# A hint at the head of every engine's program, for the branch over a fallback path

## The chip, the cores and the metric

The kernel runs on one core of one Trainium2 chip. A core has five engines that each run their own list of instructions: TensorE (PE in the profile), VectorE (DVE), ScalarE (ACT), GpSimd (POOL) and SyncE (SP).[...] The metric is the device time of one execution in microseconds (us), and the median over several runs counts.

## The reference

The first half is a linear attention with a complex, gated state. For each of 4 x 8 heads and each of 768 time steps, a state of 48 x 48 is multiplied by a complex gate of modulus at most 0.999, the outer product of a key and a value is added, and the query reads the real part:

```python
for t in range(S):
    new_re = ar * S_re - ai * S_im
    new_im = ar * S_im + ai * S_re
    S_re, S_im = (new_re + kv, new_im)
    y[:, :, t] = np.einsum('bhd,bhde->bhe', q[:, :, t], S_re)
```

The second half takes y as 3072 tokens of 384 numbers through a feed-forward layer with 2048 hidden numbers and the activation h * erf(softplus(h)):

```python
h = x @ w_in
sp = np.maximum(h, 0.0) + np.log1p(np.exp(-np.abs(h)))
g = h * erf(sp)
return (g @ w_out).astype(np.float32)
```

## The kernel before

The program holds two complete ways to the result. The fast one, `quotient_path` (line 682), replaces the recurrence by quotients of running products of the gates, so that it becomes matrix products; this is only good while certain sums over the data stay within limits. The general one, `product_path` (line 172), has no such condition. The fast path always runs. While it runs it collects sums into small tiles, and its step `check()` (line 1305) turns them into one integer, `ok`, which is 1 when all limits hold (the last operation is a reduction on DVE at line 1321). After the fast path every engine loads `ok` into a register (line 1388) and compares it (line 1389): if it is below 1, the general path runs and overwrites the output; otherwise the engines jump over it. With this input `ok` is 1, and none of the general path's instructions runs.

The fast path treats the tokens in 12 units of 256, each as two chunks of 128 rows. For a unit it loads gates, queries, keys and values, computes the gates' magnitudes, angles and decays, the scores and the state, then the first matrix product into `h` (line 1152), the activation (lines 786 and 1180 to 1186) and the second product (line 1220, and for the later units a form with seven instead of eight half-size products, line 1244). The result of a unit goes to the memory by two writes on SP's queue (line 1211). The order of all these steps is written out by hand in one long string, `ORDER` (line 49), and a scheduler leaves it as it is. It ends with the last products of unit 11 on PE, the last additions on DVE (line 1252) and the two last writes by SP; `check()` is spread over the last part of it.

At the head of the program the engines pass a barrier (line 1405), and then each begins its part of the fast path: SP and ACT issue the first loads (line 802), POOL builds an identity and a triangle, PE runs products of the identity with itself that nobody reads (line 1302).

In each engine's list the instructions stand in this order: the head, the fast path, the load of `ok` and the compare, the general path, a short piece for the other side of the condition, and the common end. The general path is 245 instructions on SP, 957 on ACT, 2537 on DVE, 743 on POOL and 4270 on PE. The short piece for the other side advances semaphores by what the general path would have added to them: one semaphore instruction on each engine but SP, and eight on SP, one for each semaphore that its transfers use. Each of these first waits until the fast path's own count is reached; SP's seventh is the one that the last write of the result increments. The common end (line 1416) has eight more semaphore waits on SP and two barriers in which POOL waits for the four other engines and releases them.

## Time and profile before

| what | value |
|---|---|
| median of 3 runs | 662.15 us (661.24 to 662.20) |
| profiled execution, its own time | 662.76 us |
| its span, from the first to the last instruction | 660.9 us |
| granted TensorE clock | 0.998 |
| busy share of the span: PE, DVE, ACT, POOL | 97%, 91%, 87%, 0% |

The span runs from the first to the last instruction of the program; what lies around it, 1.8 us, is the start and end of an execution. A busy time counts arithmetic only: semaphore instructions, register loads, branches and the issuing of transfers are listed as rows, with their times, but are not counted as busy. Engines' own instruction streams come through transfers too; the profile lists them as queues of the kind "instruction" (q8 and q14).

### The profile page before, as it was taken

The numbers are of one execution on the slowest core, as the hardware profiler recorded it, in microseconds if no ns is written. First come the engines' busy times: TensorE is split into PE (matmuls) and PEld (weight loads), VectorE is DVE, ScalarE is ACT, GpSimd is POOL, SyncE is SP. The second block draws the span as 40 slices with busy tenths as digits, with TensorE's granted clock in tenths as the row PEclk, the third lists the DMA queues.
The fourth block names the chain that finished last, engine by engine and source line by source line (L and its number), as shares of the span: only waits on it lengthen the run. The fifth ranks groups of instructions, "written<-read, shape, count | busy, mean of one in ns | idle before, by whom it ended". The sixth has DMA issues, their size and how long they took to land.

```text
span 660.9 us, 12302 instructions
## 1 busy us (share of the span) xinstructions
PE 642.7 (97%) x4728; PEld 562.4 (85%) x4728; DVE 603.3 (91%) x980; ACT 577.8 (87%) x762; POOL 1.1 (0%) x8
## 2 busy tenths in 40 slices
PE   7889999999999999999999999999999999999996
PEld 7678887777777877999899899999999899998886
DVE  4999999999999999999999999999999898877892
ACT  6999999999999999987978999997997886788810
POOL 0000000000000000000000000000000000000000
PEclk9999999999999999999999999999999999999999
DMA  8896785563157327328516726626637505511000
GB/s 197 202 266 155 188 168 120 137 127 61 24 88 132 61 37 183 70 41 199 97 17 162 145 42 151 121 39 153 119 58 144 127 16 128 136 37 48 1 25 30
DMA packets 282796, 70.23 MB, mean 106 GB/s; under 512 B 269396, under 2 KB 272488, under 8 KB 282728
## 3 DMA queue, kind: packets, MB, share of 16 engines
q1 hardware_dynamic: 280648, 68.96, 48.3%
q8 instruction: 39, 0.64, 0.4%
q10 hardware_dynamic: 2080, 0.39, 0.3%
q14 instruction: 29, 0.24, 0.1%
HBM read 48.82 MB, written 4.75 MB: 81 GB/s over the span
## 4 chain that ended last, share of the span: by engine, by line
ACT 47%; DVE 26%; PE 18%; DMA 4%; issue 4%; SPq 0%; ACTq 0%; DVEq 0%
ACT L785 10%; ACT yy L786 8%; PE hps L1152 8%; ACT z L786 7%; DVE z L1180 4%; DVE yy L1182 4%; ACT e L786 4%; DVE e L1184 4%; ACT y L786 3%; DVE h L1186 3%; ACT th L786 3%; ACT CS L786 3%; ACT h L1155 3%; PE Y L1244 2%; ACT s L786 2%
## 5 line engine op out<-in xcount | busy, mean ns | idle before, releaser
L1152 PE MATMUL hps<-xT,w_in_sb 128*128 128x256 f32 x1152 | 262.5, 381 | 1.5 <-ACT h L1155 1.5
L1152 PEld LDWEIGHTS hps<-xT,w_in_sb 128*128 128x128 f32 x1152 | 215.6, 190 | 34.8 <-ACT h L1155 4.0
L785 ACT ACT_TABLE_LOAD x94 | 120.6, 1283 | 3.6 <-issue 2.1
L1180 DVE TENSOR_TENSOR z<-z,yy 128x512 f32<-128x512 f32 x96 | 64.8, 686 | 15.8 <-ACT e L786 14.8
L786 ACT ACTIVATE e<-z 128x512 f32<-128x512 f32 x96 | 58.2, 628 | 22.1 <-DVE h L1186 21.6
L1182 DVE SCALAR_TENSOR_TENSOR yy<-z,yy 128x512 f32<-128x512 f32 x96 | 65.1, 687 | 1.7
L1186 DVE SCALAR_TENSOR_TENSOR h<-e,h 128x512 f32<-128x512 f32 x96 | 65.0, 685 | 1.1
L1220 PE MATMUL ops<-w_out_sb,h 128*128 128x384 f32 x192 | 65.7, 488 | 0.1
L1184 DVE TENSOR_TENSOR e<-e,yy 128x512 f32<-128x512 f32 x96 | 64.6, 685 | 1.1
L1155 ACT COPY h<-hps 128x512 f32<-128x512 f32 x96 | 54.6, 579 | 11.0 <-PE hps L1152 11.0
L1220 PEld LDWEIGHTS ops<-w_out_sb,h 128*128 128x128 f32 x192 | 35.7, 190 | 21.9 <-DVE w_out_sb L848 1.1
L786 ACT ACTIVATE z<-h 128x2048 f32<-128x2048 f32 x24 | 45.8, 1910 | 6.7 <-DVE seen L858 6.0
L1084 PEld LDWEIGHTS sc<-KQ 96*128 96x128 f32 x384 | 47.6, 192 | 4.4 <-issue 2.3
L1084 PE MATMUL sc<-KQ 96*128 96x128 f32 x384 | 48.9, 275 | 1.3 <-DVE KQ L1075 0.9
L786 ACT ACTIVATE z<-z 128x2048 f32<-128x2048 f32 x24 | 45.9, 1910 | 0.6
L786 ACT ACTIVATE yy<-yy 128x2048 f32<-128x2048 f32 x24 | 45.9, 1912 | 0.5
L786 ACT ACTIVATE yy<-z 128x2048 f32<-128x2048 f32 x24 | 45.8, 1908 | 0.4
L1139 PE MATMUL y<-A,v 128*32 128x128 f32 x768 | 33.4, 275 | 1.3 <-DVE A L1088 0.9
L1088 DVE TENSOR_TENSOR A<-sc,triu 128x512 f32<-128x512 f32 x48 | 31.9, 681 | 1.0 <-PE sc L1084 1.0
L1103 PEld LDWEIGHTS kv<-v,kt 128*96 128x96 f32 x320 | 29.7, 165 | 1.5 <-issue 0.7
L1103 PE MATMUL kv<-v,kt 128*96 128x48 f32 x320 | 29.7, 246 | 0.0
L1244 PE MATMUL Y<-T,S 128*128 128x192 f32 x144 | 26.7, 331 | 1.8 <-DVE out L1252 1.3
(115 smaller groups left out, 1053.7 us busy)
## 6 DMA issues: line engine op xcount, KB each, us to landing
KQ<-X SPq DMA_DIRECT2D x240, 64.0 KB
raw<-in_moe_w_in_dram SPq DMA_DIRECT2D x8, 768.0 KB
raw<-in_moe_w_out_dram SPq DMA_DIRECT2D x8, 768.0 KB
again<-in_moe_w_in_dram SPq DMA_DIRECT2D x8, 768.0 KB
ar<-in_a_re_dram SPq DMA_DIRECT2D x24, 192.0 KB
k<-in_k_dram SPq DMA_DIRECT2D x24, 192.0 KB
q<-in_q_dram SPq DMA_DIRECT2D x24, 192.0 KB
v<-in_v_dram SPq DMA_DIRECT2D x48, 96.0 KB
```

Of the source, the lines that this page charges most:

```text
L785: scalar.preload_act_table_set(sets[0])
L786: scalar.activation(func=func, **kw)
L1084: nc.tensor.matmul(out=ps[:, j, :], lhsT=head("k", g * HG + j, u, c), rhs=head("q", g * HG + j, u, c), start=True, stop=True)
L1103: nc.tensor.matmul(out=kv[0:D2, j, :], lhsT=T["kt", u, c][:, j].rearrange("p u d -> p (u d)"), rhs=side(T["v", u][:, c, j // 2], j % 2), s ...
L1152: nc.tensor.matmul(out=ps[:, e, :], lhsT=w_in_sb[:, (sl * SLAB + i) // 2, kd, e * P:(e + 1) * P], rhs=T["xT", u][:, kd, :], start=(kd == 0 ...
L1155: scalar.copy(out=T["h", u, sl][:, i:i + 2, :], in_=ps)
L1180: vector.tensor_tensor(out=z, in0=z, in1=y, op=OP.mult)
L1182: vector.scalar_tensor_tensor(out=y, in0=z, scalar=-2.0, in1=y, op0=OP.add, op1=OP.mult)
L1184: vector.tensor_tensor(out=e, in0=e, in1=y, op=OP.mult)
L1186: vector.scalar_tensor_tensor(out=h, in0=e, scalar=1.0 / RT2, in1=h, op0=OP.add, op1=OP.mult)
L1220: nc.tensor.matmul(out=ps, lhsT=lhsT, rhs=w_out_sb[:, i, :], start=i == HALF, stop=i == KF - 1)
L1244: nc.tensor.matmul(out=ps, lhsT=a(sl)[:, i], rhs=b(sl, i), start=sl == 0 and i == 0, stop=sl == NSL - 1 and i == HALF - 1)
```

## The change

Two lines are added ahead of the load of `ok`, and the condition gets a label that ties them to it:

```diff
         quotient_path(tc, q, k, v, a_re, a_im, w_in, w_out, out, ok)
+        engines = [getattr(mybir.EngineType, e) for e in ("PE", "DVE", "SP", "Activation", "Pool")]
+        tc.mark_branch_hint_location("general", hint="LikelyTaken", engines=engines)
         fine = nc.values_load(ok[0:1, 0:1], min_val=0, max_val=1)
-        with tc.If(fine < 1):
+        with tc.If(fine < 1, label="general"):
             product_path(tc, q, k, v, a_re, a_im, w_in, w_out, out)
```

Each of the five engines gets one more instruction, a branch prefetch hint that names its own compare at the end of the fast path and says that the branch there is likely taken. Although the line stands behind the fast path in the source, the built program has the hint right after the barrier at the head, as the first instruction of each engine's part, ahead of the first load on SP and ACT, of the first product on PE and of the first write on DVE and POOL. No other instruction is added, removed or put in another order.

## The prediction

> **What bounds the kernel now.** A branch matters where it is executed, so I read the end of the span first: the chain of waits for its last piece, then the rows of the compare's line, then SP's own waits, then the transfers in the gap that these show.

> The chain, in order of time (start, length, what), for the last 31 us:

> ```profile
> span 660.9 us, 12302 instructions
> ...
> 654.29 1.31 PE W L1244 x8
> 655.60 0.02 issue
> 655.62 0.36 DVE out L1252
> ```

> The last arithmetic ends at 655.98, but the span ends at 660.9 (660.94 in the trace): 4.96 us follow that hold no arithmetic. The rows of line 1389, with durations in ns and the first and last start in us, show what is there:

> ```profile
> L1389 SPq EVENT_SEMAPHORE  x8: 17/17/17, 659.0 to 659.6; - x8
> L1389 ACTq COMPARE_BRANCH  x1: 50/50/50, 647.7 to 647.7; - x1
> ...
> L1389 ACTq EVENT_SEMAPHORE  x1: 17/17/17, 650.1 to 650.1; - x1
> ...
> L1389 PEldq COMPARE_BRANCH  x1: 3302/3302/3302, 653.1 to 653.1; - x1
> L1389 DVEq COMPARE_BRANCH  x1: 72/72/72, 656.4 to 656.4; - x1
> L1389 SPq COMPARE_BRANCH  x1: 50/50/50, 656.4 to 656.4; - x1
> ...
> L1389 DVEq EVENT_SEMAPHORE  x1: 21/21/21, 659.5 to 659.5; - x1
> ```

> SP's compare takes 50 ns, from 656.392, and its next instruction starts at 659.029: 2.59 us of nothing. On ACT the hole is 2.40 us (647.74 to 650.15), on DVE 3.09 (656.45 to 659.54); on PE it lies inside the compare's 3.30. SP's waits say the same, put down to SP itself, and the transfers between 656.4 and 659.03 show what fills the hole (queue, packets, MB, share):

> ```profile
> SPq L1389 <- SPq L1389: 2.6, 1, 2.6
> ```

> ```profile
> q8 instruction: 1, 0.02, 2.1%
> q14 instruction: 2, 0.02, 1.5%
> ```

> The two q14 packets are 8 KB each, at 657.41 and 657.70, 0.97 and 1.25 us behind the compares of SP and DVE; the two engines go on 1.28 and 1.52 us after these have landed. That is the branch's target being fetched. From there on SP sets the end: eight semaphore instructions, eight waits, two barriers, 659.03 to 660.94. ACT, POOL and PE have branched before (650.1 to 656.4) and wait for SP in the barrier.

> [...]

> **The change, part by part.** *Five hints at the head.* No row shows one.[...] I take 0.07 us, what SP needs from one semaphore instruction to the next (659.443 to 659.508). Nothing hides it: the chain starts with ACT's load of ai, issued at 0.80 right behind the barrier, and the first ACT operation waits for a load until 4.13. From there to 655 the order is fixed and PE is 97% busy, so a late start is a late end: +0.07[...]. On POOL the hint delays the identity and with it PE's unread products; on DVE a few memsets: not on the chain.

> *The fetch that moves.* If the hint brings the target in ahead of the branch, the holes close. Is there time? [...]between 624.6 and 647.7 q14 has no packet at all[...], 23 us ahead of the first branch; PE's block before the branch came at 638.96 on q8, 14 us ahead of its compare. A target fetch takes 0.3 to 1 us. POOL's hint is 13 rows ahead of its compare and has 647 us.

> *What stands behind the hole.* SP would go on at about 656.50 in place of 659.03, but that 2.5 us isn't the gain. Its eight instructions each wait for a transfer count, and the seventh is that of the last write, issued at 656.008: its 16 increments come from 657.78, fourteen by 657.91, the last two at 658.02 and 658.17. In the run before, this instruction started at 659.508, the write long finished. After the change it would start some 0.04 after the landing, at 658.21. All that follows (the eighth, the eight waits, the barriers: 659.508 to 660.942 = 1.43 us) keeps its length, since [...]DVE, now on from 656.5, is ahead of it. So the span ends at 658.21 + 1.43 = 659.64: -1.30 us. If the landing improves, more: the write issued 1.1 us before had all increments after 1.845 us, this one after 2.158, and an 8 KB fetch of 0.33 us runs beside its last packets. Without such a collision the landing is 0.31 earlier. But the resumed engines will at once fetch the block behind the target (SP did so 0.58 us after resuming, at 659.61): at some 657.1, again beside the write. Bounds 0 and -0.31; I take -0.10. A fetch of 8 KB earlier in the span costs nothing that shows: q14 moves 29 packets in 660 us, a share of 0.1% of the engines' time.

> *What else.* [...] The 1.8 us around the span stays.

> Sum against the profiled execution: -1.30 - 0.10 + 0.07 = -1.33; its span 660.94 becomes 659.6, its own time 662.76 becomes 661.4. The median of the runs shown is 0.61 below that time; the same step from 662.15 gives **660.8 us**, with 660.5 (-1.61) and 661.0 (-1.19) as the bounds of the sizes. The three runs of before lie 0.96 apart, so I put 0.3 around these: 660.2 to 661.3.

> **Rivals.** *The hint does not reach its branch.* Between the head and the branches q8 fetches 37 blocks and q14 21; if one of these fetches makes an engine forget it, all holes stay and the hint's 0.07 is paid: 662.2. For it: nothing in the profile shows a hint that lives so long. Against: the hint names its compare, so it has what it needs to be used only there.

> *It works on SP and not on DVE.* Then DVE still goes on at 659.54, and SP's sixth wait of the end (for DVE's count, 659.96 before) is released at 659.60 in place of 659.96: -0.36, with the head 661.9. For it: DVE comes to its branch last (its load of ok waits for the last addition), against: 23 us are enough for both.

> *Slower: the fetch at once.* If the hint fetches the target as soon as it is read[...], the first crossing of a block behind the head misses and pays what a miss costs here: 2.4 us on ACT, 3.1 on DVE. The first 40 us are a chain of ACT operations without slack, so one of these is exposed in full[...]: 662.15 + 0.07 + 2.4 = 664.6; with DVE's behind it 667.7. It decides from a stall of 1.3 us on, the gain at the end. For it: the hint stands as far from the branch as it can[...].

> **How the numbers follow.** This kernel's runs tell a change from none at about 0.2%, 1.32 us. The chances: it works, 0.74; works only in part, 0.05; is lost, 0.09; slower, 0.12. The worked case lies right on that mark (-1.33): with bounds of -1.61 and -1.19 and the runs' spread, I give 0.48 to beyond it and 0.26 to short of it. So faster 0.48; within 0.2%: 0.26 + 0.05 + 0.09 = 0.40; slower 0.12. The range takes in the worked case and both cases without effect, 660.2 to 662.4, and leaves out the slower one.

> **What would show it.** Right: on line 1389 SP's semaphore instructions begin at about 656.5, some 0.1 behind its compare, with a hole in the middle of the eight until 658.2 that waits for the write; PE's compare drops from 3302 ns to some 50; the q14 packets between 656.4 and 659 belong to the block behind; first loads issued at 0.87. Lost: line 1389 as before. At once: a gap of some 2.5 us on ACT or DVE in the first 70 us, with an early extra q14 packet. I'd be wrong in size if the end of the span depends on more than the write, for example if the engine's next block is needed before the barrier and comes late.

## The result, and the profile after

The changed kernel takes 660.43 us (median of 19 runs, 659.06 to 661.52), the kernel before 661.98 us (19 runs, 660.91 to 663.02). The ratio is 0.9976, with a 95% interval of 0.9969 to 0.9983: 1.55 us lie between the medians, a little over 0.2%. The forecast was 660.8 us.

The profiled execution takes 659.36 us, its span 657.5. The page's first line, the end of the chain in order of time, and the rows of the compare's line, now 1391:

```profile
span 657.5 us, 12307 instructions
...
652.43 1.31 PE W L1244 x8
653.74 0.02 issue
653.77 0.36 DVE out L1252
```

```profile
L1391 SPq EVENT_SEMAPHORE  x8: 17/17/17, 655.1 to 656.1; - x8
L1391 ACTq COMPARE_BRANCH  x1: 68/68/68, 645.9 to 645.9; - x1
...
L1391 ACTq EVENT_SEMAPHORE  x1: 17/17/17, 646.3 to 646.3; - x1
L1391 POOLq EVENT_SEMAPHORE  x1: 17/17/17, 648.6 to 648.6; - x1
L1391 PEldq COMPARE_BRANCH  x1: 393/393/393, 651.3 to 651.3; - x1
...
L1391 SPq COMPARE_BRANCH  x1: 70/70/70, 654.5 to 654.5; - x1
L1391 DVEq EVENT_SEMAPHORE  x1: 21/21/21, 655.1 to 655.1; - x1
```

The last addition ends at 654.13 and the span 3.39 us later; before, it was 4.96. I call this stretch the tail and read it from the exact times of the trace in every run. The granted clock, 0.998 before and 1.000 now, is no cause of it: the lower records of before begin at 657.6 us, behind the last product. Counted from the end of its compare, SP's next instruction follows after 0.46 us in place of 2.59, DVE's after 0.51 in place of 3.09, ACT's after 0.42 in place of 2.40, and PE's compare takes 393 ns in place of 3302. POOL alone still has its hole, 645.9 to 648.6. SP's eight instructions now take 1.1 us, where they took 0.6: a wait has come between them. SP's own waits, and the page's count of instruction fetches, show where:

```profile
SPq L1391 <- SPq L1391: 1.1, 2, 0.6
```

```profile
q8 instruction: 38, 0.62, 0.4%
...
q14 instruction: 26, 0.21, 0.1%
```

There are two waits in place of one: 0.5 us behind the compare, and 0.6 us ahead of the seventh instruction, for the last write. The write's last increment comes 1.936 us behind the last addition and SP's instruction starts at 1.953. Four instruction blocks fewer are fetched, one on q8 (39 before) and three on q14 (29 before). Up to the first branch the counts are as before, 37 and 21. So the hint added no fetch, and what is saved is a later one, once each on PE, ACT, SP and DVE: in the runs below with a hint on SP alone or on DVE alone, q14 fetches 28 blocks, with hints on both 27, and q8 fetches 38 only where PE has a hint. The profile does not say what a block holds, so which fetch brings the target with a hint, and in place of what, is not shown. But one fetch shows a change: the last block on q14 ahead of the first branch comes at 611.6 to 613.0 us in the seven profiles with a hint on DVE, and at 622.6 to 625.2 in the six without.

The work before the tail was 1.85 us shorter in this profile than in that of before. That is taken up below.

### The profile page after: what moved, and what is told of

It is laid out like the page before. It is cut to its first block, busy times and chain, and to the rows that moved or that the text cites. A ratio compares the mean times of both kernels' runs of the same rounds, so it can differ in the third digit from the quotient of the medians.

```text
span 657.5 us, 12307 instructions
## 1 busy us (share of the span) xinstructions
PE 641.9 (98%) x4728; PEld 561.9 (85%) x4728; DVE 603.4 (92%) x980; ACT 577.5 (88%) x762; POOL 1.1 (0%) x8
## 4 chain that ended last, share of the span: by engine, by line
ACT 52%; DVE 23%; PE 16%; issue 4%; DMA 3%; SPq 1%; DVEq 0%; ACTq 0%
ACT L785 11%; ACT yy L786 9%; ACT z L786 8%; PE hps L1152 7%; ACT e L786 4%; DVE z L1180 4%; DVE yy L1182 4%; ACT y L786 4%; ACT th L786 3%; DVE e L1184 3%; ACT CS L786 3%; ACT h L1155 3%; DVE h L1186 3%; PE Y L1244 2%; ACT s L786 2%
## 5 line engine op out<-in xcount | busy, mean ns | idle before, releaser
L1244 PE MATMUL Y<-T,S 128*128 128x192 f32 x144 | 26.7, 331 | 1.7 <-DVE out L1252 1.3
```

The source lines that it names most:

```text
L1244: nc.tensor.matmul(out=ps, lhsT=a(sl)[:, i], rhs=b(sl, i), start=sl == 0 and i == 0, stop=sl == NSL - 1 and i == HALF - 1)
```

## The experiments

**Which engines' hints count.** Four kernels have the hints on some engines only. The edit is the tuple in the first added line:

```diff
-        engines = [... for e in ("PE", "DVE", "SP", "Activation", "Pool")]
+        engines = [... for e in ("DVE", "SP")]            # hints on SP and DVE
+        engines = [... for e in ("SP",)]                  # on SP
+        engines = [... for e in ("DVE",)]                 # on DVE
+        engines = [... for e in ("PE", "Activation", "Pool")]  # on the rest
```

> Hints on SP and DVE alone. I read the tail: from the end of the last addition on DVE (line 1252) to the end of the span, 4.96 us before, 3.39 with five hints. Theory (the gain is SP's and DVE's hole, closed up to the landing of the last write): tail 3.4 us, though PE's compare is back at about 3.3 us and ACT's hole at 2.4. Rival (all engines have to leave early, the barrier being what counts): tail about 5.0 us.

> A hint on SP alone. Theory: SP runs on behind its branch, passes the last write's landing, and then waits for DVE's count, which comes 3.56 us behind the last addition, as before; the rest takes 0.98 us: tail 4.6 us (4.96 before, 3.39 with five hints). Rival (SP's hole is the whole cost): tail 3.4 us.

> A hint on DVE alone. Theory: DVE goes on early and nobody is waiting for it, because SP's hole stays: tail 5.0 us, as before. Rival (DVE's later branch is what sets the end): tail at or below 4.6 us.

> Hints on PE, ACT and POOL alone. Theory: PE's compare falls from 3.30 us to about 0.4 and ACT's hole from 2.40 to about 0.4, POOL's stays near 2.6, and the tail stays at 5.0 us. Rival (the barrier waits for PE): tail below 4.9 us.

| hints on | tail, us | SP's hole | DVE's hole | PE's compare |
|---|---|---|---|---|
| none | 4.96 | 2.59 | 3.09 | 3.30 |
| none, once more | 4.98 | 2.61 | 2.90 | 3.78 |
| all five | 3.39 | 0.46 | 0.51 | 0.39 |
| SP and DVE | 3.38 | 0.46 | 0.51 | 3.38 |
| SP | 4.29 | 0.46 | 2.81 | 3.30 |
| DVE | 4.98 | 2.61 | 0.51 | 3.36 |
| PE, ACT, POOL | 5.38 | 3.01 | 2.90 | 0.39 |

Each row is one execution. Two hints do what five do. With SP's alone the tail falls by 0.7 us, 0.3 more than expected, since DVE's hole was 2.81 us in that execution and not 3.09; DVE's instruction starts 3.29 us behind the last addition, and 1.01 us follow. The waits of SP with a hint on SP alone name DVE:

```profile
SPq L1391 <- SPq L1391: 1.1, 2, 0.6
SPq L1418 <- DVEq L1391: 0.9, 1, 0.9
```

DVE's hint alone gains nothing; SP still waits behind its own compare:

```profile
SPq L1391 <- SPq L1391: 2.6, 1, 2.6
```

The three others gain nothing either. The tail of the last row is even longer than before, and the row for SP's waits shows why: without its hint, SP's hole is not always the same, 3.01 us here and 2.59 to 2.61 in the three other rows.

```profile
SPq L1391 <- SPq L1391: 3.0, 1, 3.0
```

**What the gain is cut short by.** The last write of the result is left out of the kernel before and of the changed one:

```diff
         def read_w(sl):
             scaled(part(0), bank(u, "W")[:, :HD], part(0))
             yield
-            put(u, 0)
+            if u < NU - 1:
+                put(u, 0)
             yield
```

> The kernel before, without the last of the 24 writes of the result (128 rows are left out), so that nothing lands in the tail. Theory (the gain of the hint is cut short by that write's landing): without hints SP branches early, DVE's hole is then what counts, tail 4.6 us (4.96 with the write); time 0.4 us shorter. Rival (the write's landing already counts in the kernel before): tail below 4.2 us.

> The kernel with five hints, without the last write of the result (128 rows are left out). Theory: SP then waits for the write before it, which lands 0.93 us behind the last addition, and the tail falls from 3.39 to about 2.5 us; so the hints are worth 2.1 us without the last write, 1.55 with it. Rival (the hinted branch itself, 0.4 to 0.5 us on SP, and not the landing sets the rest): tail within 0.1 us of 3.39.

Without hints the tail is 4.27 us (expected 4.6; DVE's hole was 2.79 in this execution) and the ratio to before 0.9994 (0.9985 to 1.0003). With hints it is 2.35 us (expected 2.5), the ratio 0.9960 (0.9948 to 0.9973). SP's waits, first without hints, then with:

```profile
SPq L1390 <- SPq L1390: 2.6, 1, 2.6
SPq L1417 <- PEq L1417: 0.6, 2, 0.4
SPq L1417 <- DVEq L1390: 0.4, 1, 0.4
```

```profile
SPq L1392 <- SPq L1392: 1.1, 2, 0.7
SPq L1419 <- PEq L1419: 0.6, 2, 0.4
```

Without hints SP, which has no last write to issue, branches 1.1 us earlier, and then DVE's hole is what it waits for (0.4 us, the last row of the first fence): 0.69 us of tail less, and none of it is the landing. With hints the seventh of SP's eight instructions starts 0.91 us behind the last addition in place of 1.95, and the tail loses 1.04 us. The hints are worth 1.92 us of tail without that write and 1.575 with it. The difference, 0.35 us, is not the price of the landing alone: in both kernels without the write SP also branches 1.1 us earlier, and DVE's hole was 0.3 us shorter in the one without hints than in the profile of before. What is shown is that the landing of the last write is what SP waits for once its hole is closed; without that write it waits for the one before, which lands 0.83 us behind the last addition.

**What is left of the branch.** The condition, the load of `ok` and the general path are taken out of the kernel before:

```diff
-        fine = nc.values_load(ok[0:1, 0:1], min_val=0, max_val=1)
-        with tc.If(fine < 1):
-            product_path(tc, q, k, v, a_re, a_im, w_in, w_out, out)
```

> The kernel before without the condition and without the general path (the fallback is left out), so without loads of ok and without branches: what a perfect hint could reach. Theory: SP's eight waits of the end begin at once, and from the landing of the write (1.94 us behind the last addition) the last 0.92 us follow: tail 2.9 us, time about 2.1 us below before, 0.5 us below the one with hints. Rival (the hint has already taken all that the branch costs): tail 3.3 to 3.4 us.

The tail is 2.76 us (expected 2.9), the ratio to before 0.9969 (0.9962 to 0.9976), 659.72 us: in the tail 0.62 us below the hinted kernel. In the total the two intervals overlap. What is left is not the 0.46 us behind the compare, which the landing hides: the write lands 0.06 us earlier here (1.87 us behind the last addition), SP runs one semaphore instruction between its wait for the landing and the barriers where the hinted kernel runs nine (0.51 us less), and the barriers take 0.05 us less. SP now waits for the transfer by name:

```profile
SPq L1413 <- DMA out_dram<-out: 1.3, 2, 1.1
```

**Why POOL's hint does nothing.** In the changed kernel POOL's hint and its branch are ten rows of the trace apart (the prediction had 13). Here 150 small writes more stand between them, which makes it 160:

```diff
             next(steps[nm])
+        for _ in range(150):
+            nc.gpsimd.memset(idle, 0.0)
```

> Five hints, and 150 writes of one element on POOL between its hint and its branch, so that the branch lies in another fetched block than the hint. Theory[...]: POOL's hole falls from 2.64 us to about 0.45. Rival (POOL doesn't use hints): the hole stays at 2.4 to 2.7 us. The tail stays at 3.4 us in both.

POOL's hole falls to 0.43 us, with a tail of 3.41:

```profile
L1394 POOLq COMPARE_BRANCH  x1: 65/65/65, 646.5 to 646.5; - x1
...
L1394 POOLq EVENT_SEMAPHORE  x1: 17/17/17, 647.0 to 647.0; - x1
```

So POOL uses hints, but not the one that stands ten rows ahead of its branch, where its hole is 2.64 us, though 645 us pass between the two. One block more is fetched on q14 ahead of the branch, at 10.2 us, which no other run has; it fits POOL reading on into another block. That this is why the hint works is an inference from one run, and when an engine takes up a hint is not shown; the number of rows at which the hint begins to work was not looked for.

**Half a write at the end.** With hints on SP and DVE, the half of the last write that is ready one addition earlier is sent off earlier:

```diff
-    def put(u, jj):
+    def put(u, jj, lo=0, hi=DM):
...
-        nc.sync.dma_start(out=out[t0:t0 + P, :], in_=o[:, jj * DM:(jj + 1) * DM])
+        nc.sync.dma_start(out=out[t0:t0 + P, lo:hi], in_=o[:, jj * DM + lo:jj * DM + hi])
...
             put(u, 1)                       # in read_z
+            if u == NU - 1:
+                put(u, 0, HD)
...
-            put(u, 0)                       # in read_w
+            put(u, 0, 0, HD if u == NU - 1 else DM)
```

> Hints on SP and DVE alone, and the last write of the result halved: its columns 192 to 383 are finished one addition earlier and are written right behind the write before; 128 x 192 are left for the end. Theory (from the landing of the last write on, the end is fixed): half the bytes land some 0.2 us earlier, tail 3.2 us (3.38 with hints on SP and DVE), time 0.2 us below the kernel with five hints, and 1.7 below before. Rival[...]: tail 3.4 us, no change.

> The changed kernel once more, on the same chip as the halved write. Theory: tail 3.4 us, ratio to before 0.9976; the 1.85 us by which the work before the tail was shorter in its first profile than in that of before is chance of the first loads, so the tail alone explains the ratio. Rival (the hints also shorten the work before the tail): ratio at or below 0.996.

> The kernel before once more, for a second profile. Theory: tail 4.9 to 5.4 us (SP's hole has been 2.59 to 3.01 us), and the work before the tail anywhere from 654.1 to 656.8 us, following the landing of the second of ACT's loads of ai (6.0 to 9.8 us so far). Rival (that landing is late in every execution without a hint on SP): it lands at 9.5 us or later again, and the work before the tail takes at least 655.9 us.

The last increment comes 1.65 us behind the last addition, not 1.93 as with the whole write, and the tail is 3.03 us (expected 3.2), 0.35 shorter than with hints on SP and DVE and a whole write: 0.28 from the landing, 0.07 because the last write now belongs to the eighth of SP's instructions and not to the seventh. The rival, a landing that doesn't depend on the bytes, falls: the half write moves as many packets as the whole one, 128, of 768 bytes in place of 1536, and takes 1.62 us from issue to the last increment, where the last whole write of every other profile took 1.84 to 2.16. The waits of SP behind its branch shrink accordingly:

```profile
SPq L1393 <- SPq L1393: 0.7, 2, 0.5
```

The time is 659.63 us (5 runs, ratio 0.9964, 0.9951 to 0.9978), beside 660.08 us for the changed kernel on the same chip (8 runs, ratio 0.9966, 0.9953 to 0.9979). The two intervals overlap: only its tail, not its time, stands clear of the changed kernel's.

**The work before the tail.** The changed kernel's second profile has a tail of 3.39 us and 655.58 us before it (654.13 in the first); the second profile of before has 4.98 and 654.53 (655.98 in the first). The signs are reversed, so the 1.85 us of the first pair do not repeat. The tails of either kernel repeat to 0.02 us. The ratio of the second series does not decide whether the work before the tail gets shorter too: its interval, 0.9953 to 0.9979, holds the 0.9976 that the tail alone would give and the 0.996 of the rival. In the second profile of before, the second of ACT's loads lands at 7.1 us, so the rival that it is late in every execution without a hint on SP falls.

## Why the prediction was right

*The holes.* They were the cost, and the hint closes them on SP, DVE, ACT and PE. The hint is read at 0.76 to 0.88 us and still works behind all 37 and 21 fetched blocks: the holes on SP, DVE and ACT are 0.42 to 0.51 us, and PE's compare takes 393 ns. The rivals of a lost hint and of one that works only on SP fall with the first profile. The slower rival, a target fetched at once, falls with the fetches: the counts up to the branch are the same, and the first packet on q14 comes at 27.4 us, no earlier than in the second profile of before (27.0; 28.9 in the first). That such a fetch would cost 2.4 us on ACT or more was my estimate, and that 23 us are room enough for the target was another.

*The hole isn't the gain.* The step from 2.5 us of hole to 1.30 of gain is right. SP's seventh instruction started 3.53 us behind the last addition and now starts at 1.95; the difference, 1.575, is that of the tails to 0.01 us, so what follows it kept its length, as predicted. The run with hints and without the last write confirms that it is this write that SP waits for.

*The landing.* It was the term that was mis-sized: I took -0.10, and it measured -0.25 us between the two first profiles (2.186 and 1.936 us behind the last addition). But the reason that I gave is not shown. The fetches of the resumed engines came as I had them, on q14 at 655.63 and 655.72 us, 0.57 and 0.60 behind the first instructions of SP and DVE. In the second profile of before, with the same fetches beside the write, it lands at 1.965, so the 2.186 was one late landing and not the rule: the bound of -0.31 was read from a single execution. It did not lengthen the tail of before, where SP's hole hid it. That tail follows the hole: in the four profiles with the last write and no hint on SP, the hole was 2.59 to 3.01 us and the tail 4.96 to 5.38.

*Behind the compare.* I had SP go on 0.1 us behind it; it takes 0.46 (0.42 on ACT, 0.51 on DVE), and PE's compare takes 393 ns, not some 50. So even the hinted branch is not free. It costs nothing here because the write lands 0.5 us later than the eight instructions would need (SP's sixth starts at 655.48, the last increment comes at 656.06); with a write more than that earlier it would be on the path, an estimate from these two times.

*The head.* The hint itself takes 43 to 65 ns, and ACT's first load is issued at 0.88 in place of 0.80, as the 0.07 says. SP's comes 0.12 later. What the forecast's bounds, 660.5 and 661.0, hold for the hints was my estimate; no profile of before shows it. The first ACT operation comes later than either, at 4.58 in place of 4.13 us, which the step did not foresee (see the last section). The total does not show it.

*POOL.* I expected its hint to work, since it has 647 us; it doesn't, and the run with more rows between hint and branch, where its hole falls from 2.64 to 0.43 us, shows that what was missing is distance in the list and not time. Nothing on the path depends on it.

*The sum.* -1.33 was forecast for the difference, -1.55 measured for the medians and -1.575 for the tails: -1.30, -0.25 from the landing, and -0.02 because SP goes on 0.02 and not 0.04 us behind it. That the medians and the tails agree so closely is in part luck: in the second series the medians are 2.23 us apart with the same tails. And 660.8 started from a median of 662.15 over three runs, 0.17 above that over 19. The forecast gave a change beyond 0.2% no more than 0.48, because -1.33 is just that mark; with the landing as measured it would have lain beyond it.

## What to carry to other kernels

Look for time behind the last arithmetic operation: a jump over code that isn't used cost an engine 2.4 to 3.8 us here where its hint was missing or did not work, and it was only paid on the engines for which the end of the program waited, SP and then DVE. When such a hole is to be closed, ask what is hidden in its shadow: of 2.1 us of hole that were closed on SP, 1.6 came out, because the landing of the last write took over. A hint ten rows ahead of its branch did nothing on POOL and one 160 rows ahead worked, and hints on the two late engines gave what hints on all five gave.

## What the runs showed of the hardware that was not expected

A hinted branch still takes 0.42 to 0.51 us from its compare to the next instruction, on SP, ACT, DVE and, where its hint works, POOL, and it is nearly the same in all runs (0.458 or 0.459 on SP in six kernels).

With SP's first load issued 0.12 us later, the first loads land at other times. These are the first loads and ACT's first operations that need them, before and after (start, length, what, and the idle time ahead of it):

```profile
0.80 1.25 ACTq L802 DMA_DIRECT2D ai<-in_a_im_dram  x2
0.80 1.08 SPq L802 DMA_DIRECT2D ar<-in_a_re_dram  x2
4.13 0.52 ACT L786 ACTIVATE th<-ar 128x384 f32<-128x384 f32 x1 [0.77 <-DMA ar<-in_a_re_dram]
...
9.82 0.52 ACT L786 ACTIVATE y<-ai 128x384 f32<-128x384 f32 x1 [2.12 <-DMA ai<-in_a_im_dram]
```

```profile
0.88 1.14 ACTq L802 DMA_DIRECT2D ai<-in_a_im_dram  x2
0.92 1.23 SPq L802 DMA_DIRECT2D ar<-in_a_re_dram  x2
4.58 0.52 ACT L786 ACTIVATE th<-ar 128x384 f32<-128x384 f32 x1 [1.25 <-DMA ar<-in_a_re_dram]
...
8.04 0.51 ACT L786 ACTIVATE y<-ai 128x384 f32<-128x384 f32 x1
```

In the seven profiles with a hint on SP, the second of ACT's loads has landed at 5.9 to 6.6 us; in the six without, at 6.4 to 9.8, twice over 9.6. Four runs separate the loads. In the three with a hint on SP and none on ACT, only SP's first load is delayed (0.92, ACT's stays at 0.80), and ACT's second load lands at 5.95 to 6.04; with hints on PE, ACT and POOL, only ACT's is (0.88, SP's stays at 0.80), and it lands at 6.40. So the delay of SP's load alone goes with the early landing; no run shows the reason. The work before the tail is 654.8 us on average in the former and 655.4 in the latter, and the two profiles in which the load landed after 9.6 us have the longest (655.98 and 656.82). But single profiles range from 654.1 to 656.8, so whether the change gains from this too stays open.
